# A new load split and new instruction orders for the start and the end of a fused attention and MLP kernel

## The chip, the cores and the metric

The kernel runs on one core of a Trainium2 chip (trn2). The metric is the device time of one execution in microseconds (us). Before the change it was 283.31 us, the median of three executions (282.98 to 283.46).

The engines are called by the profile's short names: PE is TensorE's matmuls and PEld its weight loads, DVE is VectorE, ACT is ScalarE, POOL is GpSimd, SP is SyncE (here it only issues DMA).

## The reference

```python
def _attn_ref(q, k, v):                       # each (8, 8, 576, 64): batch, head, row, head_dim
    q_s = softmax of q over head_dim          # max taken off first, 1e-9 added to the sum
    k_s = softmax of k over the rows
    kv = np.einsum('bhsd,bhse->bhde', k_s, v)
    return np.einsum('bhsd,bhde->bhse', q_s, kv)

def _moe_ref(x, w_in, w_out, beta):           # x (4608, 512), w_in (512, 2048), w_out (2048, 512)
    h = x @ w_in
    g = h * (1.0 / (1.0 + np.exp(-beta * h)))
    return g @ w_out
```

The attention output of all batches, as 4608 rows of 512, is the x of the second part. The inputs are float32. The kernel computes in bfloat16 with float32 accumulation.

## The kernel before

The program takes the rows in nine chunks. Chunks 0 to 7 are the first 512 rows of each batch, and one more chunk holds the 64 rows that are left of every batch. For a chunk the kernel makes qT (softmaxed q, transposed), one small matrix kv for each pair of heads, and x = kv times qT. Then 16 units follow. A unit j is 128 of the 2048 hidden columns: four matmuls for h (kt 0 to 3), a tanh on ACT, a product g on DVE, and four matmuls of g with w_out into four accumulators. So h and acc take 64 matmuls each in a chunk.

The program hands every engine its instructions in the order in which they are written. For batches 0 and 1 that order was tuned by hand, because weights, q, k and v arrive while the first products run. These are the parts that the change and the argument touch:

```python
    def load_q(b, parts=1, only=None, eng=nc.sync):
        # ... tile, source ...
        for s in range(parts) if only is None else (only,):
            eng.dma_start(t[:, s * n : (s + 1) * n, :], src[:, s * n : (s + 1) * n, :])

    # q_exp: ACT exponential of a group of heads; q_sum: DVE sum and reciprocal; q_mul: DVE product
    # tpe: four PE transposes of a head pair; q_ev: their eviction to qT; vz_cast: v to bfloat16
    # kz_exp: ACT exponential of k of a pair; kvz_norm: DVE reciprocal and two products
    def kvz_mm(b, j, tag=None, n=1):          # kv of head pair j: 18 products of 64x64 tiles
        # ...
        for i in range(RW):                   # 9
            for e in range(2):
                r = slice(e * D, (e + 1) * D)
                nc.tensor.matmul(t[r, 0, :], ek[b][r, j, ds(i * D, D)], va[b][r, j, i, :],
                                 start=(i == 0), stop=(i == RW - 1), tile_position=(e * D, e * D))

    def warm(n, tag):                         # n dummy matmuls on zeros
        # ...

    load_q(0, 2, 0)                           # 4 heads on SyncE's queue
    load_q(0, 2, 1, nc.scalar)                # 4 heads on ScalarE's
    load_kv(k_st, k, 0, "k_st", whole=True)
    # ... v of batch 0 by pair, beta, then the weights by block ...

    warm(18, tag="b0")
    q_exp(0, 0)
    q_sum(0, 0)
    q_exp(0, 1)
    q_mul(0, 0)
    kz_exp(0, 0)
    kz_exp(0, 1)
    q_sum(0, 1)
    vz_cast(0, 0, G)
    warm(18, tag="acc2")
    tpe(0, 0, "acc3")
    tpe(0, 1, "acc2")
    # ... batch 0 goes on; then, in batch 1:
    tpe(1, 0, "b0")
    w_cast("out", 3, 0, A)
    tpe(1, 1, "b1")
    kvz_mm(1, 0, "b2", 2)                     # two pairs in a row
    q_ev(1, 1, V)
    kvz_mm(1, 1)
    # ...
    mm_b(0, 14)
    vz_cast(1, 2, A, part=1)
    vz_cast(1, 2, G, part=0)
    kvz_mm(1, 3, "b0", 1)                     # two pairs in a row
    kvz_mm(1, 2, "b1", 1)
    # ...
    for st in range(R + 1):                   # the end: units 8 to 15 of the last chunk
        for j in range(HOLD, NJ):
            mm_b(LASTC, j, [st])
        store(LASTC, st)
```

The softmax here doesn't subtract the row's maximum and nothing guards it: scores larger than these inputs give would overflow.

## Time and profile before

| | before |
|---|---|
| time, median of 3 | 283.31 us |
| span of the profiled execution | 281.1 us (its time 282.86 us) |
| PE busy | 273.4 us, 97% |
| useful PE work starts | 10.29 us |
| h runs in one go, but for one stall, from | 16.02 us |

From the page of the kernel before come PE's line of the busy times and the chain of waits by engine:

```profile
PE 273.4 (97%) x1705; PEld 128.4 (46%) x1734; DVE 172.4 (61%) x269; ACT 162.9 (58%) x249; POOL 37.0 (13%) x57
PE 91%; DMA 6%; issue 1%; SPq 1%; POOL 0%; ACT 0%
```

PE bounds the kernel. In its steady part matmuls of 512 columns start every 0.216 us, and the change makes none of them shorter. Time can be won only where PE waits or does something useless.

The timeline of PE in the kernel before follows. Its columns are start in us, length in us, engine, line, operation, output and inputs, form, and how many instructions are merged; a bracket gives the idle time in front and what ended it. Now and then one matmul's record is missing, as in the run of 15 at 36.29, which has 16 in the program.

```profile
1.19 9.27 PE L518 MATMUL warm<-xT 128*128 128x512 bf16 x36 [1.19 <-DVE xT L599]
10.29 0.61 PE L294 MATMUL tp<-identity,eq 128*128 128x128 bf16 x8
...
16.02 3.40 PE L397 MATMUL h<-xT,w_in_b 128*128 128x512 bf16 x15
19.66 2.55 PE L397 MATMUL h<-xT,w_in_b 128*128 128x512 bf16 x11 [0.24 <-POOL w_in_b L170]
22.04 3.62 PE L445 MATMUL acc<-w_out_b,g 128*128 128x512 bf16 x16
...
36.29 3.62 PE L445 MATMUL acc<-w_out_b,g 128*128 128x512 bf16 x15
...
40.28 0.77 PE L313 MATMUL kv<-va,ek 64*64 64x65 bf16 x36
...
42.73 1.89 PE L445 MATMUL acc<-w_out_b,g 128*128 128x512 bf16 x8
44.55 0.77 PE L313 MATMUL kv<-va,ek 64*64 64x65 bf16 x36
...
46.99 3.19 PE L397 MATMUL h<-xT,w_in_b 128*128 128x512 bf16 x14
```

At 36.29 us PE has done all 64 h matmuls and 32 of the 64 acc matmuls of chunk 0. I call this milestone 1. At 46.99 us it starts the run of 14 h matmuls of chunk 1, with everything of chunk 0 and of batch 1's attention behind it. I call this milestone 2. The same work is done at these points in every kernel below. Between the milestones lie the other 32 acc matmuls, 16 transposes, the kv products of batch 1, four x and two h.

One weight load in the timeline of PEld of the kernel before:

```profile
44.55 0.65 PEld L313 LDWEIGHTS <-ek 64*64 64x64 bf16 x36 [0.42 <-ACT va L168]
```

PEld was idle for 0.42 us there and waited for a cast on ACT. The printed length of a run reaches about 0.16 us into the next one.

The end of the kernel before, from the timeline of PEld:

```profile
272.35 3.35 PEld L445 LDWEIGHTS <-g 128*128 128x128 bf16 x17 [0.48 <-DVE g L411]
```

The eighth of the last acc matmuls needs the last g, which DVE finishes at 272.30 us. From the start of the last h matmul to the first of the last 16 half-width products it took 5.56 us, where 24 matmuls at 0.216 us take 5.18 and the last h itself 0.22 us, so about 0.16 us was lost.

### The profile page before, as it was taken

What the parts mean: (1) busy time and instruction counts of PE and PEld (TensorE: products, weight loads), DVE (VectorE), ACT (ScalarE), POOL (GpSimd) and SP (SyncE); (2) the same over time, 40 slices, a digit from 0 to 9 for tenths busy, and PEclk for the clock granted to TensorE, in tenths of its full rate; (3) what the DMA queues carried; (4) which work ended last, traced back from release to release, by engine and by line L of the source; (5) the groups of instructions that cost most, each with busy time, mean ns of one, the idle gap of its engine ahead of it and who ended that gap; (6) DMA issues with size and microseconds to landing.
All of it is one profiled execution on the core that took longest, in us unless ns stands there. A gap on an engine that the chain in (4) does not pass through costs nothing.

```text
span 281.1 us, 4410 instructions
## 1 busy us (share of the span) xinstructions
PE 273.4 (97%) x1705; PEld 128.4 (46%) x1734; DVE 172.4 (61%) x269; ACT 162.9 (58%) x249; POOL 37.0 (13%) x57
## 2 busy tenths in 40 slices
PE   8899999999999999999999999999999999999995
PEld 3544454444444444444444444444444544445543
DVE  1864785983498338934794469546964596454361
ACT  3777886953495339633873478337933574354451
POOL 1551436230030003000300030001200000000000
PEclk9999999999999999999999999999999999999999
DMA  6999999929942994099409940698153034005003
GB/s 243 391 392 392 384 392 314 295 58 259 232 169 35 261 265 155 8 285 266 155 0 217 326 156 16 138 247 252 75 126 102 6 146 75 0 0 152 0 0 149
DMA packets 55172, 50.09 MB, mean 178 GB/s; under 512 B 26600, under 2 KB 47344, under 8 KB 55152
## 3 DMA queue, kind: packets, MB, share of 16 engines
q1 hardware_dynamic: 54480, 49.17, 58.5%
q10 hardware_dynamic: 672, 0.66, 0.7%
q8 instruction: 13, 0.21, 0.3%
q14 instruction: 7, 0.06, 0.1%
HBM read 36.71 MB, written 9.44 MB: 164 GB/s over the span
## 4 chain that ended last, share of the span: by engine, by line
PE 91%; DMA 6%; issue 1%; SPq 1%; POOL 0%; ACT 0%
PE acc L445 43%; PE h L397 43%; DMA v_st<-in_v_dram 3%; DMA w_in<-in_moe_w_in_dram 3%; PE kv L338 2%; PE x L369 1%; PE acc L437 1%; PE kv L313 0%; PE tp L294 0%; PE x L382 0%; POOL w_in_b L170 0%; SPq L131 0%; SPq L128 0%; SPq L105 0%; SPq L150 0%
## 5 line engine op out<-in xcount | busy, mean ns | idle before, releaser
L407 ACT ACTIVATE th<-h,beta_t 128x512 bf16<-128x512 f32 x144 | 97.6, 686 | 87.9 <-PE h L397 85.8
L411 DVE SCALAR_TENSOR_TENSOR g<-th,h 128x512 bf16<-128x512 bf16 x144 | 96.7, 680 | 83.2 <-ACT th L407 81.4
L397 PE MATMUL h<-xT,w_in_b 128*128 128x512 bf16 x569 | 141.1, 379 | 0.6 <-POOL w_in_b L170 0.2
L445 PE MATMUL acc<-w_out_b,g 128*128 128x512 bf16 x538 | 136.1, 379 | 2.0 <-issue 1.3
L397 PEld LDWEIGHTS <-w_in_b 128*128 128x128 bf16 x576 | 56.3, 98 | 66.6 <-POOL w_in_b L170 0.7
L445 PEld LDWEIGHTS <-g 128*128 128x128 bf16 x560 | 53.5, 98 | 65.6 <-issue 2.5
L170 POOL CAST va<-v_st 128x2048 bf16<-128x2048 f32 (+2 forms) x14 | 16.9, 1205 | 145.3 <-DMA v_st<-in_v_dram 145.1
L258 DVE TENSOR_REDUCE rq<-eq 128x16 f32<-128x1024 bf16 x18 | 21.9, 1216 | 7.5 <-ACT eq L247 7.1
L264 DVE TENSOR_TENSOR eq<-eq,rq 128x1024 bf16<-128x1024 bf16 x18 | 22.5, 1248 | 0.1
L247 ACT ACTIVATE eq<-q_st 128x1024 bf16<-128x1024 f32 x16 | 16.6, 1053 | 3.2 <-DMA q_st<-in_q_dram 3.2
L168 ACT CAST xT<-x 128x512 bf16<-128x512 f32 x18 | 9.9, 589 | 11.1 <-PE x L369 10.1
L170 DVE CAST xT<-x 128x512 bf16<-128x512 f32 x18 | 11.8, 687 | 6.1 <-PE x L369 5.3
L170 DVE COPY o<-acc 128x512 f32<-128x512 f32 (+1 forms) x19 | 12.1, 669 | 3.4 <-PE acc L445 3.2
L168 ACT COPY o<-acc 128x512 f32<-128x512 f32 (+1 forms) x18 | 9.6, 576 | 7.1 <-PE acc L445 2.9
L189 ACT ACTIVATE ek<-k_st 128x1024 bf16<-128x1024 f32 x12 | 12.6, 1052 | 0.0
L518 PE MATMUL warm<-xT 128*128 128x512 bf16 x36 | 9.3, 423 | 1.2 <-DVE xT L599 1.2
L170 POOL CAST w_in_b<-w_in 128x512 bf16<-128x512 f32 (+1 forms) x10 | 6.8, 698 | 8.6 <-DMA w_in<-in_moe_w_in_dram 8.6
L518 PEld LDWEIGHTS <-xT 128*128 128x128 bf16 x36 | 3.8, 107 | 6.2 <-issue 1.8
L182 ACT ACTIVATE ek<-k_st 128x576 bf16<-128x576 f32 x8 | 5.3, 684 | 1.5 <-DMA k_st<-in_k_dram 1.5
L168 ACT CAST w_out_b<-w_out 128x1024 bf16<-128x1024 f32 x5 | 5.3, 1051 | 0.2 <-DMA w_out<-in_moe_w_out_dram 0.2
L338 PEld LDWEIGHTS <-ek 128*64 128x64 bf16 x192 | 4.1, 111 | 2.5 <-issue 2.5
L437 PE MATMUL acc<-w_out_b,g 128*128 128x256 bf16 x32 | 5.0, 273 | 0.0
(48 smaller groups left out, 79.6 us busy)
## 6 DMA issues: line engine op xcount, KB each, us to landing
out_dram<-o SPq DMA_DIRECT2D x14, 512.0 KB, 3.7
q_st<-in_q_dram SPq DMA_DIRECT2D x24, 256.0 KB, 4.2
k_st<-in_k_dram SPq DMA_DIRECT2D x6, 1024.0 KB, 8.3
v_st<-in_v_dram SPq DMA_DIRECT2D x6, 1024.0 KB, 11.0
w_in<-in_moe_w_in_dram SPq DMA_DIRECT2D x6, 512.0 KB, 9.4
v_st<-in_v_dram SPq DMA_DIRECT2D x8, 288.0 KB, 8.2
w_out<-in_moe_w_out_dram SPq DMA_DIRECT2D x4, 512.0 KB, 9.2
w_out<-in_moe_w_out_dram SPq DMA_DIRECT2D x2, 1024.0 KB, 10.6
```

The source lines that it names most:

```text
L168: eng.copy(dst, src)
L170: eng.tensor_copy(dst, src)
L189: nc.scalar.activation(ek[b][:, :, h, :].rearrange("p i h d -> p h i d"), k_st[b][:, h, 0 : R * D].rearrange("p h (i d) -> p h i d", i=R), ...
L247: nc.scalar.activation(eq[b][:, :, s * m : (s + 1) * m, :].rearrange("p i h d -> p h i d"), q_st[b][:, s * m : (s + 1) * m, :].rearrange(" ...
L258: nc.vector.tensor_reduce(rq[b][:, 0, :, h], eq[b][:, :, h, :], axis=AX.X, op=ALU.add)
L264: eng.tensor_tensor(eq[b][:, :, h, :], eq[b][:, :, h, :], rq[b][:, 1, :, h].unsqueeze(3).to_broadcast((P, R, m, D)), ALU.mult,)
L338: nc.tensor.matmul(t[r * D : (r + 1) * D, j, :], ek[b][:, i, hd, :] if i < R else ekt[(b // 2) % 2][:, ds(hd * D, D)], va[b][:, i, hd, :] ...
L397: nc.tensor.matmul(h[:], w_unit(j, kt), x_of(c)[:, kt, :], start=(kt == 0), stop=(kt == KT - 1),)
L407: nc.scalar.activation(th[:], h_of[c, j][:], ACTF.Tanh, scale=beta_t[:, j : j + 1])
L411: nc.vector.scalar_tensor_tensor(out=g[:], in0=th_of.pop((c, j))[:], scalar=1.0, in1=h_of[c, j][:], op0=ALU.add, op1=ALU.mult)
L445: nc.tensor.matmul(acc[st][:], g[:, ds(st * P, P)], w_out_b[:, j, :], start=(j == 0), stop=(j == NJ - 1),)
L518: nc.tensor.matmul(t[:], xT[2][:, 0, 0:P], xT[2][:, 0, :])
```

## The change

The change has four parts. Head: q of batch 0 comes as one head pair on SyncE's queue and three pairs on ScalarE's, its softmax goes pair by pair, and batch 0 gets a new order (with 30 dummy matmuls instead of 36, in four groups). Weight loads: input block 3 comes before output block 1. Batch 1: a new order, with each pair's kv product alone, and new loads to match. Tail: unit 15 is used one matmul later.

```diff
-        for s in range(parts) if only is None else (only,):
-            eng.dma_start(t[:, s * n : (s + 1) * n, :], src[:, s * n : (s + 1) * n, :])
+        only = range(parts) if only is None else only
+        hs = slice(n * only[0], n * (only[-1] + 1))
+        eng.dma_start(t[:, hs, :], src[:, hs, :])
...
-    HB, AB = ["b0", "b1"], ["b2", "b3"]
+    HB, AB = ["b1", "b2"], ["b0", "b3"]
...
-    load_q(0, 2, 0)
-    load_q(0, 2, 1, nc.scalar)
+    load_q(0, 4, [0])
+    load_q(0, 4, [1, 2, 3], nc.scalar)
...
-    w_load("out", 1)
     w_load("in", 3, 1)
     w_load("in", 3, 0)
+    w_load("out", 1)
... (new order of the k and v loads of batch 1)
-    q_exp(0, 0)
-    q_sum(0, 0)
-    q_exp(0, 1)
-    q_mul(0, 0)
+    q_exp(0, 0, 4)
+    q_sum(0, 0, 4)
+    q_exp(0, 3, 4)
+    q_mul(0, 0, 4)
+    q_exp(0, 2, 4)
+    q_sum(0, 3, 4)
+    tpe(0, 0, "acc3")
+    q_exp(0, 1, 4)
+    q_sum(0, 2, 4)
+    q_ev(0, 0, A)
+    q_sum(0, 1, 4)
+    q_mul(0, 2, 4)
     kz_exp(0, 0)
+    q_mul(0, 1, 4)
+    warm(10, tag="acc2")
+    tpe(0, 2, "acc3")
     kz_exp(0, 1)
... (the rest of batch 0 in a new order)
-    kvz_mm(1, 0, "b2", 2)
-    q_ev(1, 1, V)
-    kvz_mm(1, 1)
+    kvz_mm(1, 0, "b1", 1)
+    kz_exp(1, 2)
+    tpe(1, 3, "b3")
+    kvz_norm(1, 0)
+    tpe(1, 2, "b2")
     mm_b(0, 12)
+    kz_exp(1, 1)
+    q_ev(1, 3, V)
+    q_ev(1, 2, V)
+    kvz_mm(1, 2, "b0", 1)
... (kv of pair 1 after one x, kv of pair 3 after mm_b(0, 14))
-    for st in range(R + 1):
-        for j in range(HOLD, NJ):
+    for j in range(HOLD, NJ - 1):
+        mm_b(LASTC, j, [0])
+    mm_b(LASTC, HOLD, [1])
+    mm_b(LASTC, NJ - 1, [0])
+    store(LASTC, 0)
+    for st in range(1, R + 1):
+        for j in range(HOLD + (st == 1), NJ):
             mm_b(LASTC, j, [st])
         store(LASTC, st)
```

The intent is that h starts earlier, that less waits for the last data of batch 1, and that the last g is waited for no more. The arithmetic is the same.

More of the change, by code (lines that the diff above doesn't have):

```diff
@@ L565 @@
     load_kv(v_st, v, 0, "v_st", [1])
+    load_kv(v_st, v, 0, "v_st", [2])
     nc.sync.dma_start(beta_r[:], moe_beta.rearrange("(hh q) -> hh q", q=2 * P))
-    load_kv(v_st, v, 0, "v_st", [2])
     load_kv(v_st, v, 0, "v_st", [3])
@@ L578 @@
     w_load("in", 2, 1)
-    w_load("out", 1)
     w_load("in", 3, 1)
     w_load("in", 3, 0)
-    load_q(1, 2, 0)
+    w_load("out", 1)
+    load_q(1, 2, [0])
     w_load("out", 2)
-    load_q(1, 2, 1)
-    load_kv(v_st, v, 1, "v_st", [1])
+    load_q(1, 2, [1])
+    load_kv(v_st, v, 1, "v_st", [2])
+    w_load("out", 3, 0)
     load_kv(k_st, k, 1, "k_st", [0])
     load_kv(v_st, v, 1, "v_st", [0])
+    load_kv(k_st, k, 1, "k_st", [2])
     load_kv(k_st, k, 1, "k_st", [1])
-    w_load("out", 3, 0)
+    load_kv(v_st, v, 1, "v_st", [1])
     w_load("out", 3, 1)
-    load_kv(k_st, k, 1, "k_st", [2])
+    load_kv(k_st, k, 1, "k_st", [3])
     load_kv(v_st, v, 1, "v_st", [3])
-    load_kv(k_st, k, 1, "k_st", [3])
-    load_kv(v_st, v, 1, "v_st", [2])
     load_q(2)
@@ L605 @@
     warm(18, tag="b0")
-    q_exp(0, 0)
-    q_sum(0, 0)
-    q_exp(0, 1)
-    q_mul(0, 0)
+    q_exp(0, 0, 4)
[10 more added lines that the diff above has]
+    q_mul(0, 2, 4)
     kz_exp(0, 0)
+    q_mul(0, 1, 4)
+    warm(10, tag="acc2")
+    tpe(0, 2, "acc3")
     kz_exp(0, 1)
-    q_sum(0, 1)
+    q_ev(0, 2, V)
     vz_cast(0, 0, G)
-    warm(18, tag="acc2")
@@ L616 @@
-    tpe(0, 0, "acc3")
+    warm(1, tag="acc1")
     tpe(0, 1, "acc2")
-    q_ev(0, 0, A)
-    kvz_mm(0, 0, "acc1", 1)
+    q_mul(0, 3, 4)
+    kz_exp(0, 2)
+    warm(1, tag="acc1")
+    kvz_mm(0, 0, "acc3", 1)
     vz_cast(0, 1, G)
+    q_ev(0, 1, V)
+    tpe(0, 3, "acc1")
     kz_exp(0, 3)
+    kvz_norm(0, 0)
+    kvz_mm(0, 1, "acc2", 1)
+    vz_cast(0, 2, G)
+    q_ev(0, 3, A)
     beta_pe("acc0")
-    kvz_norm(0, 0)
-    kvz_mm(0, 1, "acc3", 1)
-    vz_cast(0, 2, G)
-    kz_exp(0, 2)
-    q_mul(0, 1)
@@ L628 @@
-    xpe(0, 0, "b3")
+    kvz_norm(0, 1)
+    kvz_mm(0, 2, "acc3", 1)
+    vz_cast(0, 3, A, part=1)
+    vz_cast(0, 3, G, part=0)
     beta_ev()
-    vz_cast(0, 3, G, part=0)
-    vz_cast(0, 3, A, part=1)
-    kvz_mm(0, 2, "acc1", 2)
+    xpe(0, 0, "acc1")
+    kvz_norm(0, 2)
+    kvz_mm(0, 3, "acc2", 1)
+    w_castk(0, 0, G)
     xev(0, 0, A)
-    kvz_mm(0, 3)
-    w_castk(0, 0, G)
-    q_ev(0, 1, A)
-    kvz_norm(0, 1)
-    tpe(0, 3, "acc0")
-    tpe(0, 2, "b3")
-    w_castk(0, 1, G)
-    q_ev(0, 3, A)
@@ L642 @@
-    hpe(0, 3, [0], "b0")
-    kvz_norm(0, 2, 2)
-    xpe(0, 1, "acc3")
-    hpe(0, 1, [0], "b1")
-    q_ev(0, 2, A)
-    hpe(0, 2, [0], "b2")
-    xev(0, 1, V)
-    hpe(0, 0, [0], "acc0")
-    w_castk(0, 2, A)
-    xpe(0, 3, "acc2")
+    xpe(0, 1, "acc0")
+    kvz_norm(0, 3)
+    xpe(0, 2, "b3")
+    xev(0, 1, A)
+    hpe(0, 0, [0], "b0")
+    hpe(0, 1, [0], "b1")
+    xev(0, 2, V)
+    w_castk(0, 1, A)
+    xpe(0, 3, "acc3")
+    w_castk(0, 2, G)
+    hpe(0, 3, [0], "b2")
+    xev(0, 3, V)
+    hpe(0, 2, [0], "acc0")
@@ L652 @@
+    hpe(0, 0, [1])
     w_castk(0, 3, G)
-    xpe(0, 2, "acc1")
-    xev(0, 3, V)
-    hpe(0, 0, [1])
-    xev(0, 2, A)
+    hpe(0, 3, [1])
+    hpe(0, 3, [2])
     hpe(0, 1, [1])
-    hpe(0, 3, [1])
-    hpe(0, 2, [1])
-    hpe(0, 2, [2])
-    hpe(0, 2, [3])
+    hpe(0, 1, [2])
+    hpe(0, 1, [3])
+    hpe(0, 3, [3])
+    th_act(0, 1)
     w_castk(1, 0, G)
     hpe(0, 0, [2])
-    th_act(0, 2)
-    hpe(0, 1, [2])
-    w_castk(1, 1, G)
-    hpe(0, 1, [3])
-    hpe(0, 5, [0], "b3")
-    th_act(0, 1)
@@ L670 @@
-    hpe(0, 3, [2])
-    g_dve(0, 2)
-    hpe(0, 5, [1])
-    w_castk(1, 2, G)
-    hpe(0, 3, [3])
-    w_castk(1, 3, A)
-    hpe(0, 0, [3])
-    g_dve(0, 1)
-    hpe(0, 6, [0], "b2")
-    hpe(0, 5, [2])
-    th_act(0, 3)
-    hpe(0, 5, [3])
-    hpe(0, 7, [0], "b1")
-    th_act(0, 0)
+    hpe(0, 0, [3])
+    hpe(0, 2, [1])
+    w_castk(1, 1, G)
+    th_act(0, 3)
+    hpe(0, 2, [2])
+    g_dve(0, 1)
+    hpe(0, 2, [3])
+    hpe(0, 4, [0], "b3")
+    th_act(0, 0)
+    hpe(0, 4, [1])
+    g_dve(0, 3)
@@ L684 @@
+    w_castk(1, 3, G)
+    hpe(0, 5, [0], "b1")
+    hpe(0, 5, [1])
+    w_castk(1, 2, A)
+    g_dve(0, 0)
+    hpe(0, 7, [0], "b2")
+    th_act(0, 2)
+    hpe(0, 7, [1])
+    hpe(0, 4, [2])
+    hpe(0, 5, [2])
+    hpe(0, 4, [3])
+    g_dve(0, 2)
+    hpe(0, 5, [3])
+    th_act(0, 4)
+    hpe(0, 7, [2])
+    hpe(0, 7, [3])
+    hpe(0, 6, [0], "b0")
+    w_cast("out", 0, 0, G)
+    th_act(0, 5)
     hpe(0, 6, [1])
-    g_dve(0, 3)
+    g_dve(0, 4)
     hpe(0, 6, [2])
     hpe(0, 6, [3])
-    th_act(0, 5)
@@ L689 @@
-    w_cast("out", 0, 0, G)
-    hpe(0, 7, [1])
-    g_dve(0, 0)
-    hpe(0, 7, [2])
-    hpe(0, 4, [0], "b0")
-    th_act(0, 6)
-    g_dve(0, 5)
-    hpe(0, 4, [1])
-    hpe(0, 4, [2])
-    mm_b(0, 0)
-    w_cast("out", 0, 1, A)
+    th_act(0, 7)
+    g_dve(0, 5)
+    mm_b(0, 0)
+    th_act(0, 6)
+    w_cast("out", 0, 1, G)
+    g_dve(0, 7)
+    mm_b(0, 1)
     g_dve(0, 6)
-    mm_b(0, 1)
-    w_castk(2, 0, G)
+    w_castk(2, 0, A)
+    w_castk(2, 1, G)
     mm_b(0, 2)
-    w_castk(2, 1, G)
     mm_b(0, 3)
@@ L706 @@
     w_castk(2, 2, A)
-    w_castk(2, 3, A)
-    hpe(0, 4, [3])
-    hpe(0, 7, [3])
-    th_act(0, 4)
-    hpe(0, 9, [0, 1, 2, 3], "b2")
-    th_act(0, 7)
-    g_dve(0, 4)
-    hpe(0, 8, [0, 1, 2, 3], "b3")
+    w_castk(2, 3, G)
+    hpe(0, 11, [0, 1, 2, 3], "b0")
+    w_cast("in", 3, 1, A)
+    hpe(0, 10, [0, 1, 2, 3], "b1")
+    th_act(0, 11)
+    hpe(0, 8, [0, 1, 2, 3], "b2")
+    w_cast("in", 3, 0, G)
+    th_act(0, 10)
+    g_dve(0, 11)
+    hpe(0, 9, [0, 1, 2, 3], "b3")
+    th_act(0, 8)
+    g_dve(0, 10)
@@ L715 @@
+    hpe(0, 13, [0, 1, 2, 3], "b0")
+    g_dve(0, 8)
     th_act(0, 9)
-    g_dve(0, 7)
-    w_cast("out", 1, 0, A)
-    hpe(0, 11, [0, 1, 2, 3], "b0")
+    hpe(0, 14, [0, 1, 2, 3], "b1")
     g_dve(0, 9)
-    hpe(0, 10, [0, 1, 2, 3], "b1")
-    th_act(0, 8)
-    w_cast("in", 3, 1, G)
-    th_act(0, 11)
-    g_dve(0, 8)
+    th_act(0, 13)
+    w_cast("out", 1, 0, G)
+    w_cast("out", 1, 1, A)
+    hpe(0, 15, [0, 1, 2, 3], "b2")
+    g_dve(0, 13)
     mm_b(0, 4)
-    w_cast("out", 1, 1, A)
-    g_dve(0, 11)
@@ L728 @@
-    w_cast("in", 3, 0, G)
+    th_act(0, 14)
+    th_act(0, 15)
+    g_dve(0, 14)
     mm_b(0, 5)
-    th_act(0, 10)
+    q_exp(1, 0)
+    g_dve(0, 15)
     mm_b(0, 6)
-    g_dve(0, 10)
-    q_exp(1, 0)
-    hpe(0, 13, [0, 1, 2, 3], "b0")
     q_sum(1, 0)
-    hpe(0, 12, [0, 1, 2, 3], "b1")
-    th_act(0, 13)
     mm_b(0, 7)
-    th_act(0, 12)
-    g_dve(0, 13)
-    w_cast("out", 2, 1, G)
-    w_cast("out", 2, 0, A)
-    hpe(0, 14, [0, 1, 2, 3], "b2")
-    q_mul(1, 0)
-    hpe(0, 15, [0, 1, 2, 3], "b0")
@@ L746 @@
-    q_exp(1, 1)
-    g_dve(0, 12)
-    mm_b(0, 8)
-    vz_cast(1, 1, G)
-    th_act(0, 14)
-    q_sum(1, 1)
-    th_act(0, 15)
-    mm_b(0, 9)
-    kz_exp(1, 0)
-    vz_cast(1, 0, G, part=0)
-    mm_b(0, 10)
-    g_dve(0, 15)
-    vz_cast(1, 0, A, part=1)
-    kz_exp(1, 1)
-    g_dve(0, 14)
-    mm_b(0, 11)
-    q_mul(1, 1)
-    tpe(1, 0, "b0")
-    w_cast("out", 3, 0, A)
-    tpe(1, 1, "b1")
-    kvz_mm(1, 0, "b2", 2)
-    q_ev(1, 1, V)
-    kvz_mm(1, 1)
-    q_ev(1, 0, A)
-    tpe(1, 3, "b1")
@@ L771 @@
-    kvz_norm(1, 0, 2)
-    tpe(1, 2, "b3")
-    w_cast("out", 3, 1, G)
-    mm_b(0, 12)
-    q_ev(1, 2, A)
-    q_ev(1, 3, V)
-    kz_exp(1, 2)
-    xpe(1, 1, "b0")
-    xpe(1, 0, "b1")
-    xev(1, 1, V)
-    mm_b(0, 13)
+    w_cast("out", 2, 1, A)
+    w_cast("out", 2, 0, G)
+    hpe(0, 12, [0, 1, 2, 3], "b0")
+    q_mul(1, 0)
+    q_exp(1, 1)
+    mm_b(0, 8)
+    vz_cast(1, 2, G, part=0)
+    vz_cast(1, 2, A, part=1)
+    mm_b(0, 9)
+    q_sum(1, 1)
+    th_act(0, 12)
+    tpe(1, 0, "b1")
+    w_cast("out", 3, 0, A)
@@ new lines @@
+    tpe(1, 1, "b2")
+    mm_b(0, 10)
+    q_ev(1, 0, V)
+    q_mul(1, 1)
+    kz_exp(1, 0)
+    mm_b(0, 11)
+    vz_cast(1, 0, G, part=0)
+    vz_cast(1, 0, A, part=1)
+    q_ev(1, 1, A)
+    g_dve(0, 12)
+    kvz_mm(1, 0, "b1", 1)
[3 more added lines that the diff above has]
+    tpe(1, 2, "b2")
+    mm_b(0, 12)
+    kz_exp(1, 1)
+    q_ev(1, 3, V)
+    q_ev(1, 2, V)
+    kvz_mm(1, 2, "b0", 1)
+    vz_cast(1, 1, A, part=1)
+    vz_cast(1, 1, G, part=0)
+    xpe(1, 0, "b1")
+    kvz_norm(1, 2)
@@ L782 @@
+    kvz_mm(1, 1, "b2", 1)
+    xev(1, 0, A)
+    mm_b(0, 13)
+    kvz_norm(1, 1)
+    w_cast("out", 3, 1, G)
+    hpe(1, 0, [0], "b0")
+    xpe(1, 2, "b1")
+    kz_exp(1, 3)
+    xpe(1, 1, "b2")
+    xev(1, 2, V)
+    mm_b(0, 14)
     vz_cast(1, 3, A, part=1)
     vz_cast(1, 3, G, part=0)
-    xev(1, 0, A)
-    kz_exp(1, 3)
-    mm_b(0, 14)
-    vz_cast(1, 2, A, part=1)
-    vz_cast(1, 2, G, part=0)
-    kvz_mm(1, 3, "b0", 1)
-    kvz_mm(1, 2, "b1", 1)
+    xev(1, 1, V)
+    kvz_mm(1, 3, "b1", 1)
@@ L791 @@
+    mm_b(0, 15)
     kvz_norm(1, 3)
-    mm_b(0, 15)
-    kvz_norm(1, 2)
-    xpe(1, 3, "b0")
+    hpe(1, 2, [0], "b2")
     store(0, 0)
-    hpe(1, 0, [0], "b2")
-    xev(1, 3, V)
-    hpe(1, 0, [1])
-    xpe(1, 2, "b1")
-    hpe(1, 1, [0], "b3")
-    store(0, 1)
-    xev(1, 2, A)
-    hpe(1, 1, [1])
-    hpe(1, 2, [0], "b0")
-    hpe(1, 2, [1])
+    xpe(1, 3, "b1")
+    hpe(1, 1, [0], "b3")
+    hpe(1, 1, [1])
+    xev(1, 3, A)
+    store(0, 1)
+    hpe(1, 1, [2])
+    hpe(1, 0, [1])
     hpe(1, 0, [2])
+    hpe(1, 0, [3])
@@ L807 @@
     store(0, 2)
-    hpe(1, 0, [3])
-    hpe(1, 1, [2])
+    hpe(1, 1, [3])
+    hpe(1, 3, [0], "b1")
+    th_act(1, 0)
     store(0, 3)
-    th_act(1, 0)
-    hpe(1, 1, [3])
-    hpe(1, 2, [2])
-    hpe(1, 2, [3])
-    th_act(1, 1)
-    hpe(1, 3, [0], "b1")
-    g_dve(1, 0)
     hpe(1, 3, [1])
     hpe(1, 3, [2])
-    th_act(1, 2)
     hpe(1, 3, [3])
+    th_act(1, 1)
+    g_dve(1, 0)
+    hpe(1, 2, [1])
+    hpe(1, 2, [2])
+    th_act(1, 3)
+    hpe(1, 2, [3])
     g_dve(1, 1)
     mm_b(1, 0)
-    th_act(1, 3)
+    th_act(1, 2)
@@ L825 @@
+    g_dve(1, 3)
+    mm_b(1, 1)
     g_dve(1, 2)
-    mm_b(1, 1)
-    g_dve(1, 3)
     tail_zero(0)
```

## The prediction

> **What bounds the kernel now.** TensorE: 273.4 us busy of a 281.1 us span (page, busy times) and 91% of the chain of waits; DMA of v and w_in at the start makes up most of the rest. From about 50 us the timeline shows matmuls back to back at 216 ns, which the change hardly touches. What can be won lies in the first 50 us and the last 10.
>
> Head (timeline): 36 dummy matmuls hold TensorE until 10.3 us; from there to 16.0 us it issues about 4.2 us of useful work (transposes, k-v products, x, 3 h), so about 1.5 us is idle; only then does h run gaplessly. It stalls 0.24 us at 19.4 us (weight block 1, second half) and about 0.35 us near 44.2 us, where the last v pair of batch 1 landed at 43.7 us. DMA is full until 44 us (390 GB/s), so arrivals are a floor for any reordering.
>
> Tail: the weight load waits 0.48 us for the last g; TensorE loses about 0.15 us.
>
> **What the change does.**
> 1. q as 2+6 heads. In the DMA packets SyncE's queue moves alone for 1.25 us (200 KB), then each queue gets about 190 KB/us, half of one alone. This agrees with the Trainium skill, "DMA: Bandwidth & Descriptors", section on queues, rings and completion order: an engine takes turns between queues. Estimate: the first pair lands at about 4.0 us (half of q landed at 5.6), the other three at 6.8 (was 6.2). k (9.2 us) and v (from 10.0) stay.
> 2. Softmax by pair: reductions and products (1.22 us for 4 heads) become about 0.63 us each. VectorE also gets two evictions (0.42 us). Estimate: its k-v normalisations end near 15.5 us (was 14.95), the last x eviction near 16.8 (as now). VectorE becomes the tight engine of the head.
> 3. All q is transposed before the last k-v product, so h starts earlier (about 14.6 us) and fills the wait: 22 h matmuls instead of 18 by 19.6 us. Lead: 0.5 to 0.9 us.
> 4. Weight block 3 before output block 1: neutral.
> 5. Batch 1: one pair instead of two waits for the last data; a k-v pair (0.36 us), x (0.22) and h (0.22) run before it. This hides the 0.35 us stall.
> 6. Last unit last in the first block: one 216 ns matmul covers the wait; saves about 0.15 us.
>
> **Sum.** Lead 0.7, plus 0.35, plus 0.15, minus about 0.3 for new waits among small pieces: about 1.0 us, all on the critical path. The arrival at 43.7 us caps it at about 1.4 us.
>
> Predicted time 282.3 us, 8 in 10 between 281.5 and 283.1. Faster by over 2%: 0.01; within 2%: 0.98; slower by over 2%: 0.01.
>
> **What would show it.** First q exponential near 4.2 us, the next near 6.9; first h near 14.6 us, 22 by 19.6; first output product near 21.8 us (was 22.04); no TensorE gap near 44 us; the k-v product of batch 1's last pair near 44.2 us; no wait for g at the end; steady state unchanged.
>
> **What would make it wrong.** If the six heads land after 7.5 us, VectorE pushes the last x eviction past 17.5 us and the lead vanishes. In-order ScalarE holds casts waiting for DMA in front of evictions; one late landing at 36 to 42 us could cost 0.5 us. With fewer dummy matmuls, gaps could slow TensorE (the first dummies took 0.43 us, later ones 0.216): the clock row of the slices would show under 9 early on.

## The result, and the profile after

| | before | after |
|---|---|---|
| median | 283.38 us (4 executions, 282.98 to 283.56) | 282.56 us (4 executions, 282.47 to 282.69) |
| ratio | | 0.9973, 95% interval 0.9956 to 0.9991 |
| span of the profiled execution | 281.1 us (time 282.86) | 280.8 us (time 282.55) |

A ratio here is the mean time of one kernel's executions over that of the other's of the same rounds, so it is not quite the ratio of the medians quoted. Executions over 1.5% slower than the fastest of the same kernel are left out of the means. The output is correct.

The gain is 0.82 us by the medians and 0.3 us by the two traces. The difference between these two numbers comes up again below: the traced execution of the kernel before (282.86 us) was faster than each of the four timed with it.

From the page of the kernel after:

```profile
PE 273.9 (98%) x1699; PEld 128.2 (46%) x1728; DVE 175.3 (62%) x284; ACT 162.0 (58%) x248; POOL 38.7 (14%) x58
PE 94%; DMA 3%; issue 1%; POOL 1%; SPq 0%; ACT 0%
```

The timeline of PE after:

```profile
1.19 6.67 PE L519 MATMUL warm<-xT 128*128 128x512 bf16 x18 [1.19 <-DVE xT L600]
7.69 0.39 PE L295 MATMUL tp<-identity,eq 128*128 128x128 bf16 x4
7.92 2.32 PE L519 MATMUL warm<-xT 128*128 128x512 bf16 x10
...
14.42 0.38 PE L398 MATMUL h<-xT,w_in_b 128*128 128x512 bf16 x1
...
15.07 6.88 PE L398 MATMUL h<-xT,w_in_b 128*128 128x512 bf16 x30
21.78 3.62 PE L446 MATMUL acc<-w_out_b,g 128*128 128x512 bf16 x16
...
35.60 1.89 PE L446 MATMUL acc<-w_out_b,g 128*128 128x512 bf16 x7
...
39.67 0.48 PE L314 MATMUL kv<-va,ek 64*64 64x65 bf16 x18
...
41.49 0.48 PE L314 MATMUL kv<-va,ek 64*64 64x65 bf16 x18
...
42.22 0.48 PE L314 MATMUL kv<-va,ek 64*64 64x65 bf16 x18
...
45.11 0.48 PE L314 MATMUL kv<-va,ek 64*64 64x65 bf16 x18
...
46.83 3.19 PE L398 MATMUL h<-xT,w_in_b 128*128 128x512 bf16 x14
```

Read it against the list of before. The dummies are split, so the first transposes run at 7.69 us. From 15.07 us h runs to the first acc at 21.78 us. By the starts of its matmuls it loses 0.06 us at 15.57 us and 0.17 us at 19.20 us, in front of weight loads; the kernel before lost 0.41 us at 19.66 us (the 0.24 us of the list is counted from the printed end). So the stall is shorter, not gone. By then all 32 h matmuls of units 0 to 7 are done, where before had 30. Milestone 1 is at 35.60 us instead of 36.29, a lead of 0.69 us. Milestone 2 is at 46.83 us instead of 46.99, and the lead has shrunk to 0.16 us. So 0.53 us were lost again between the milestones, in batch 1, where the prediction expected a further gain of 0.35 us.

The first two exponentials of q on ACT, after the change, show when the first pair and the other three had landed:

```profile
3.79 0.63 ACT L248 ACTIVATE eq<-q_st 128x512 bf16<-128x512 f32 x1 [1.25 <-DMA q_st<-in_q_dram]
6.13 1.67 ACT L248 ACTIVATE eq<-q_st 128x512 bf16<-128x512 f32 x3 [1.70 <-DMA q_st<-in_q_dram]
```

Before, the first exponential ran at 5.68 us.

The same weight load at the end, after:

```profile
272.19 3.19 PEld L446 LDWEIGHTS <-g 128*128 128x128 bf16 x16 [0.27 <-DVE g L412]
```

From the start of the last h matmul to the first of the last 16 half-width products it now took 5.40 us instead of 5.56: the tail order saves 0.16 us. PEld still waits a little for g, but PE has no gap there.

### The profile page after: what moved, and what is told of

Its sections match the earlier page's. It is cut to its first block, busy times and chain, and to the rows that moved or that the text cites. A ratio compares the mean times of both kernels' runs of the same rounds, so it can differ in the third digit from the quotient of the medians.

```text
span 280.8 us, 4419 instructions
## 1 busy us (share of the span) xinstructions
PE 273.9 (98%) x1699; PEld 128.2 (46%) x1728; DVE 175.3 (62%) x284; ACT 162.0 (58%) x248; POOL 38.7 (14%) x58
## 4 chain that ended last, share of the span: by engine, by line
PE 94%; DMA 3%; issue 1%; POOL 1%; SPq 0%; ACT 0%
PE h L398 44%; PE acc L446 43%; DMA v_st<-in_v_dram 3%; PE kv L339 2%; PE x L370 1%; PE acc L438 1%; PE kv L314 1%; PE x L383 1%; POOL va L171 1%; PE tp L295 0%; SPq L129 0%; SPq L106 0%; ACT o L169 0%; PE x L361 0%; PE tb L552 0%
## 5 line engine op out<-in xcount | busy, mean ns | idle before, releaser
L171 POOL CAST va<-v_st 128x2048 bf16<-128x2048 f32 (+2 forms) x14 | 17.5, 1261 | 145.7 <-DMA v_st<-in_v_dram 145.7
L259 DVE TENSOR_REDUCE rq<-eq 128x16 f32<-128x1024 bf16 (+1 forms) x20 | 22.1, 1105 | 5.6 <-ACT eq L248 5.2
L265 DVE TENSOR_TENSOR eq<-eq,rq 128x1024 bf16<-128x1024 bf16 (+1 forms) x20 | 22.8, 1142 | 0.1
L248 ACT ACTIVATE eq<-q_st 128x1024 bf16<-128x1024 f32 (+1 forms) x18 | 16.9, 956 | 3.2 <-DMA q_st<-in_q_dram 3.2
L171 POOL CAST w_in_b<-w_in 128x512 bf16<-128x512 f32 (+1 forms) x9 | 5.9, 660 | 5.7 <-DMA w_in<-in_moe_w_in_dram 5.6
L171 POOL CAST w_out_b<-w_out 128x1024 bf16<-128x1024 f32 x5 | 5.2, 1040 | 6.3 <-DMA w_out<-in_moe_w_out_dram 6.3
L260 DVE RECIPROCAL rq<-rq 128x16 f32<-128x16 f32 (+1 forms) x20 | 4.9, 243 | 0.7
```

The costliest lines, as they stand in the source:

```text
L171: eng.tensor_copy(dst, src)
L248: nc.scalar.activation(eq[b][:, :, s * m : (s + 1) * m, :].rearrange("p i h d -> p h i d"), q_st[b][:, s * m : (s + 1) * m, :].rearrange(" ...
L259: nc.vector.tensor_reduce(rq[b][:, 0, :, h], eq[b][:, :, h, :], axis=AX.X, op=ALU.add)
L265: eng.tensor_tensor(eq[b][:, :, h, :], eq[b][:, :, h, :], rq[b][:, 1, :, h].unsqueeze(3).to_broadcast((P, R, m, D)), ALU.mult,)
```

## The experiments

Twelve runs followed, three of them repeats. Each had five rounds, with the kernel before in the same rounds. The rounds came in three groups: before_again, before_tail, head_only and batch1_only; then head_tail, grouped, fewer_dummies and q_4_4, on another chip; then the other four, on the chip of the first group. Between groups, compare the ratios to the kernel before and the traces rather than the medians. All of them except one execution, named below, were of state fast, and all outputs were correct.

The table gives, for each profiled execution, milestone 1, the stretch from milestone 1 to milestone 2, and the rest from milestone 2 to the end of the span. The starts were read from the timeline of PE as above.

| kernel | median, us | milestone 1 | stretch | rest |
|---|---|---|---|---|
| before | 283.38 | 36.29 | 10.70 | 234.10 |
| before_again | 283.15 | 36.26 | 10.70 | 234.10 |
| before_tail | 283.18 | 36.76 | 10.70 | 233.93 |
| batch1_only | 283.55 | 36.42 | 11.24 | 234.09 |
| fewer_dummies | 284.29 | 37.61 | 10.70 | 234.09 |
| after | 282.56 | 35.60 | 11.23 | 233.92 |
| grouped | 283.09 | 35.57 | 11.79 | 233.93 |
| q_4_4 | 284.22 | 37.38 | 11.14 | 233.93 |
| head_only | 282.15 | 35.47 | 10.77 | 234.10 |
| head_tail | 282.11 | 35.49 | 10.99 | 233.93 |
| head_tail_again | 282.21 | 35.84 | 10.79 | 233.92 |
| mul_early | 282.39 | 36.05 | 10.71 | 233.92 |
| no_mid_dummies | 284.46 | 35.52 | 10.71 | 233.93 |

The rest is one of two numbers: 234.10 with the old tail and 233.93 with the new one, within 0.01 us. Everything else is decided before milestone 2.

### before_again: the kernel before, unchanged

> The kernel before once more, unchanged, for the spread and a second trace of it. Both theories: ratio 1.000 within 0.001. Theory A (before has no slack at its last k-v pair of batch 1: data ready 44.47 us, TensorE there at 44.46 us in the first trace): executions differ by some 0.5 us, and in a slower execution the extra time lies before that pair, as a TensorE wait there or in the head. Rival: the spread lies anywhere, or in the start and end.

Measured: 283.15 us (282.85 to 283.95, six executions), ratio 1.0004 (0.9990 to 1.0019). The eleven executions of the kernel before in the same rounds went from 282.63 to 283.59. So the kernel before differs from itself by about 1 us. Its second trace is as fast as the first and shows no place for the spread; the next experiment does by chance. What I called a lack of slack at the last kv pair turned out wrong (see head_only).

### before_tail: the tail order alone

```diff
 (on the kernel before)
-    for st in range(R + 1):
-        for j in range(HOLD, NJ):
+    ... the new last loop of the change
```

> Only the last part of the change (unit 15 after one matmul of block 1). From the traces of before and after: the last 16 half-width products start 0.18 us nearer to the last h than before, so 0.15 to 0.2 us less, about 283.2 us; the weight load still waits for g for about 0.3 us instead of 0.5. Rival (end is set by stores): no difference.

Measured: 283.18 us, ratio 0.9995 (0.9982 to 1.0008). The timed difference is not clear of noise. The trace shows the 0.17 us that was expected (rest 233.93 instead of 234.10), and milestone 1 of this execution is 0.47 us later, which has nothing to do with the tail. Its timeline of PE shows why:

```profile
1.19 10.39 PE L518 MATMUL warm<-xT 128*128 128x512 bf16 x36 [1.19 <-DVE xT L599]
11.41 0.61 PE L294 MATMUL tp<-identity,eq 128*128 128x128 bf16 x8
```

The same 36 dummies took 10.39 us here and 9.27 us in the first trace. In this execution 12 of the first 17 distances between their starts were about 0.4 us, in the first one 6; the later ones were 0.216 us. The record of the granted clock says full speed from 6.17 us here and from 3.90 us there. The old head puts all dummies in front of the first transposes, so a late clock pushes the first transposes from 10.29 to 11.41 us. In batch1_only, with full clock from 5.04 us, they started at 10.86 us. The Trainium skill, "TensorE: Matmul & The Clock Gate", Part 1, says that the clock is raised after a window of about 3.4 us of activity, and that the window runs free, so that the point differs from run to run. The traces agree with that: full speed began between 3.90 and 7.23 us in the traces that have this record, a spread of 3.33 us.

### head_only: the new head, with the old batch 1 and the old tail

```diff
 (on the changed kernel; loads of batch 1, bank sets and last loop as before)
-    hpe(0, 12, [0, 1, 2, 3], "b0")
+    hpe(0, 12, [0, 1, 2, 3], "b3")
... batch 1 as in the kernel before: kvz_mm(1, 0) and (1, 1) in a row, (1, 3) and (1, 2) in a row
```

> New q split and new batch 0, old order of batch 1 and old tail. Theory A (the head's lead of 0.69 us at 36 us is real, but batch 1's last k-v pair waits for data that land at 43.7 us): TensorE reaches that pair at about 43.8 us, waits until about 44.5 us for the casts, and the lead at 50 us is 0.0 to 0.15 us; time equal to before within 0.2 us. Theory B (the single k-v bursts of the new batch 1 are what eats the lead, 0.52 us by the trace): without them the lead stays 0.6 to 0.7 us, time 0.6 us below before.

Measured: 282.15 us (282.12 to 283.08), ratio 0.9969 (0.9956 to 0.9983). Theory A falls and theory B holds; the gain, 0.9 us by the ratio, is larger than the 0.6 us of theory B. The timeline of PE of this run:

```profile
35.47 3.62 PE L446 MATMUL acc<-w_out_b,g 128*128 128x512 bf16 x16
...
39.46 0.77 PE L314 MATMUL kv<-va,ek 64*64 64x65 bf16 x36
...
43.73 0.84 PE L314 MATMUL kv<-va,ek 64*64 64x65 bf16 x36
...
46.24 3.18 PE L398 MATMUL h<-xT,w_in_b 128*128 128x512 bf16 x14
```

The lead of 0.82 us at milestone 1 is still 0.75 us at milestone 2. The last kv group ran 0.82 us earlier than before and took only 0.07 us longer. In the first trace the cast that this group needs ended at 44.47 us, and I took that for a limit set by the landing of v at 43.60 us. It was not: an x eviction of PE's results and an exponential stood in front of the cast on ACT, so its time followed PE's pace. With a faster PE the cast ended at 43.96 us, with v landed at 43.53. That is close to the real limit: this run waited 0.07 us for it and the next ones up to 0.29 us.

### batch1_only: the new order of batch 1 alone

```diff
 (on the kernel before; its loads of batch 1 and bank sets as after)
-    ... batch 1 of the kernel before
+    ... batch 1 of the changed kernel: kvz_mm(1, 0), (1, 2), (1, 1), (1, 3), each alone
```

> Old head, new order of batch 1 (four single k-v bursts, new loads of batch 1), old tail. Theory A and the burst account: four single bursts take 0.41 us each plus a 0.1 us drain in front of each instead of two pairs of 0.70 us, so TensorE is 0.4 to 0.5 us behind before at 50 us, and the time is 0.3 to 0.5 us above before, unless before itself waits there in its slower executions. Rival (the new order of batch 1 gains by hiding a wait of 0.35 us, as predicted): 0.3 us below before.

Measured: 283.55 us (283.35 to 284.56), ratio 1.0019 (1.0004 to 1.0034). The stretch is 11.24 us, as in the changed kernel, and not 10.70. So the new order of batch 1 costs 0.54 us of PE time, and it costs that with the old head as well as with the new one. The timeline of PE of this run gives the account of it:

```profile
41.37 1.03 PE L445 MATMUL acc<-w_out_b,g 128*128 128x512 bf16 x4
42.33 0.48 PE L313 MATMUL kv<-va,ek 64*64 64x65 bf16 x18
42.73 0.39 PE L382 MATMUL x<-qsT,kvp 128*128 128x512 bf16 x1
43.05 0.48 PE L313 MATMUL kv<-va,ek 64*64 64x65 bf16 x18
```

Four acc matmuls fill 0.863 us where h or acc follows them. Here they start at 41.37 us and kv starts 0.96 us later, so about 0.09 us is lost in front of the group. One x (0.216 us) is followed by kv after 0.32 us, which loses 0.10 us. A single group takes 0.41 us until the next kind of matmul starts. In the old order two groups in a row take 0.70 us together, and there is one gap in front of both. In the changed kernel the same sums are 4 times 0.41 minus 2 times 0.70, which is 0.24 us, plus about 0.28 us for the gaps (0.46 us in front of four groups, 0.18 us in front of two). Together they make 0.52 of the 0.53 us.

Not all of this is the price of the groups. The first of the four gaps is 0.17 us in the changed kernel, 0.08 us more than the others behind acc: PE waited there for POOL's cast of v, which ended at 39.62 us (it took 0.83 us under a product on DVE; the same cast took 0.46 us in q_4_4, under a sum). (In batch1_only the same 0.08 us appear behind the first group, where the transposes wait for a product on DVE.) The run q_4_4, described below, has the same order of batch 1 without this wait. Its stretch is 11.14 us, so the groups and their gaps alone cost 0.44 us. First the cast in the changed kernel, then milestones 1 and 2 of q_4_4:

```profile
38.79 0.83 POOL L171 CAST va<-v_st 128x320 bf16<-128x320 f32 x1 [2.19 <-DMA v_st<-in_v_dram]
```

```profile
37.38 1.89 PE L446 MATMUL acc<-w_out_b,g 128*128 128x512 bf16 x8
...
48.52 3.19 PE L398 MATMUL h<-xT,w_in_b 128*128 128x512 bf16 x14
```

The Trainium skill, "TensorEngine Tiling (Array Packing)", Key Properties, says that a change of tiling mode drains the engine. The traces agree: kv is the only part of this stretch that uses 64x64 tiles, and every change to it shows a gap of 0.09 us or more. The page does not give the size.

### head_tail and head_tail_again: the new head and the new tail, old batch 1

```diff
 (on the kernel of head_only)
+    ... the new last loop of the change
```

> New head of batch 0 and new tail, old order of batch 1. From the traces: the earlier run of the head alone ended 0.72 us ahead, the tail order saves 0.17 us between the last h and the last products. Theory (the two add, the new batch 1 order is a net cost): trace span near 280.2 us, median about 282.0 us, 0.4 to 0.6 us below the changed kernel. Rival (the run of the head alone was only lucky): about 282.5 us, as the changed kernel.

> New head, new tail, old order of batch 1, now in the same rounds as the changed kernel. Theory (the new order of batch 1 is a net cost of 0.4 to 0.5 us): 0.3 to 0.5 us below the changed kernel in these rounds. Rival (earlier difference was chance between rounds): within 0.15 us of it.

> The changed kernel once more, in the same rounds as the next one: median 282.4 to 282.7 us, spread about 0.3 us, and a second trace of it. In that trace the accounting of batch 1 repeats: four single k-v bursts of 0.41 us.

The first time it was 282.11 us (281.94 to 282.32), ratio 0.9965 (0.9943 to 0.9986). The second time it ran in the same rounds as the changed kernel: 282.21 us (282.08 to 282.34) against 282.59 us (282.49 to 283.00, five fast executions), with ratios to the kernel before of 0.9961 (0.9945 to 0.9978) and 0.9976 (0.9957 to 0.9995). So it beats both kernels: 0.38 us below the changed one by the medians of the same rounds, without overlap between their executions. The two intervals do overlap, since they carry the spread of the kernel before. The trace has a span of 280.41 us and not 280.2; in the stretch 0.29 us of waiting appeared at the last kv group. In the second trace it was 0.09 us, so that wait varies. Here theory A is right after all, with an earlier limit than I thought: v landed at 43.78 us, its casts ended at 44.28 us, and the second pair of the group started at 44.34 us. A still faster head would gain little in this order. The two gains did not add in the times: head_only had 282.15 us, so the 0.17 us of the tail show in the traces only.

One execution of the changed kernel in these rounds took 414.29 us, at a mean granted clock of 0.66. The profile fell on it. I compare nothing with it, and so there is no second fast trace of the changed kernel; its order of batch 1 is seen once more in q_4_4.

### grouped: three kv products of batch 1 in one group

```diff
 (on the changed kernel)
-    kvz_mm(1, 0, "b1", 1)
+    mm_b(0, 12)
     kz_exp(1, 2)
     tpe(1, 3, "b3")
-    kvz_norm(1, 0)
     tpe(1, 2, "b2")
-    mm_b(0, 12)
...
+    kvz_mm(1, 0, "b1", 1)
     kvz_mm(1, 2, "b0", 1)
-    xpe(1, 0, "b1")
     kvz_mm(1, 1, "b2", 1)
     mm_b(0, 13)
+    xpe(1, 0, "b1")
...
```

> The changed kernel with the first three k-v products of batch 1 in one burst instead of three single ones. Burst account (a single burst costs 0.41 us and a 0.1 us drain in front; in a group 0.35 us each): two bursts less, so the start of the second batch's long h run moves about 0.3 us earlier relative to the run of acc at 35 us, time 0.2 to 0.4 us below the changed kernel, about 282.2 us. Rival (batch 1 waits for data in any order): no gain, the burst itself waits.

Measured: 283.09 us (283.04 to 283.45), ratio 1.0001 (0.9979 to 1.0023), where the changed kernel had 0.9973 and 0.9976 in its own rounds. The stretch is 11.79 us instead of 11.23. This attempt failed. The 54 products take 1.20 us until acc starts, 0.18 us of it a gap in front of the third pair; without that gap a pair takes 0.34 us, as the account says. But the order around them now waits:

```profile
39.93 1.04 PE L446 MATMUL acc<-w_out_b,g 128*128 128x512 bf16 x4 [0.30 <-DVE g L412]
...
41.35 1.26 PE L314 MATMUL kv<-va,ek 64*64 64x65 bf16 x54
...
43.42 0.96 PE L383 MATMUL x<-qsT,kvp 128*128 128x512 bf16 x3
```

The acc matmuls of unit 12 came before their g was ready, and three x in a row took 1.05 us until the next matmul, where three nominal slots are 0.65 us: they wait for the three normalisations that DVE does one after the other. The waits ate more than the group saved. The run does not refute the account of the groups, but its time does not confirm the size either.

### fewer_dummies and no_mid_dummies: are the dummies needed?

```diff
 (fewer_dummies, on the kernel before)
-    warm(18, tag="acc2")
+    warm(8, tag="acc2")
 (no_mid_dummies, on the kernel of head_tail)
-    warm(10, tag="acc2")
```

> The kernel before with 26 instead of 36 dummy matmuls. Theory (TensorE starts its first transposes only when the dummies are done, and that takes 10.3 to 11.4 us depending on how many of them run at 0.43 instead of 0.216 us): the first transposes start when their data are there, at about 9.6 to 9.9 us, the spread between executions falls from about 1 us to about 0.3 us and the median by 0.1 to 0.3 us. Rival (the spread comes from the DMA or elsewhere): same spread, same median.

> As the run before last (new head and tail, old batch 1), without the 10 dummy matmuls between the first transposes and the second. Theory (they keep TensorE's granted clock up; with 26 instead of 36 dummies in the old kernel one trace showed the clock at 0.5 for 3.4 us and four of six executions were 1.3 to 2.5 us longer): in part of the executions the clock falls, median 0.5 to 2 us above its parent, spread over 1 us. Rival (transposes and k-v products suffice): same time as its parent.

Measured: 284.29 us (282.56 to 285.13), ratio 1.0032 (0.9999 to 1.0066), and 284.46 us (281.94 to 284.94), ratio 1.0033 (1.0005 to 1.0062). By these ratios only the second is clear of noise. For the first kernel my theory was wrong: the spread grew instead of shrinking. The theory drawn from that held for the second kernel. Both kernels fall into groups by the mean granted clock of the execution. At 1.00 fewer_dummies took 282.56 and 282.94 us. At 0.988 it took 284.38, 285.07 and 285.13 us, and at 0.994 284.20 us. At 1.00 no_mid_dummies took 281.94 and 282.62 us. At 0.988 it took 284.43 to 284.94 us, in four executions. The profile of fewer_dummies fell on the execution at 0.994. This is the view by windows of that run; after the busy times the columns are the granted clock, the DMA share and GB/s:

```profile
7.30:14.00 6.70, 5.36 (x93) 3.41 (x92) 5.89 (x12) 4.58 (x10) 3.61 (x5) 1.00 1.05 390
14.10:17.40 3.30, 3.30 (x22) 1.75 (x16) 1.44 (x4) 1.59 (x3) 1.98 (x5) 0.50 1.04 374
```

By the record of the clock it was at half from 14.06 to 17.47 us, which is the length of the window that the page names, and the first acc came at 23.36 us instead of 22.04. As an estimate, one stretch of 3.41 us at half speed lowers the mean over 283 us to 0.994 and two lower it to 0.988, which are the means seen. So the dummies do two jobs: they raise the clock (read from the traces; no run leaves the first ones out) and they keep it up through the thin stretch of transposes and kv products. The new head keeps the clock up with 12 dummies placed between the transposes; with 10 of them gone it fell in four of six executions. In the executions that I have of the changed kernel, head_only and head_tail, leaving out the 414 us one, the mean clock was never under 0.998. The kernel before had two executions at 0.994 among those listed in the rounds, 284.78 and 284.19 us. These are part of its spread. Whether such a drop comes in a given execution I cannot predict; the trace of no_mid_dummies shows PE busy for only 4.83 of the same 6.70 us and no drop. Counted in stretches of 3.41 us from the rise of the clock, PE was busy for 2.34 us of the one before the drop, and for 1.72 us of one in no_mid_dummies (6.82 to 10.23 us) that no drop followed. So PE's busy time alone does not decide it.

### q_4_4: the old split of q

```diff
 (on the changed kernel)
-    load_q(0, 4, [0])
-    load_q(0, 4, [1, 2, 3], nc.scalar)
+    load_q(0, 2, [0])
+    load_q(0, 2, [1], nc.scalar)
```

> The changed kernel with q of batch 0 in two halves of four heads on the two queues, as before; softmax by pair stays. Theory (the early pair lets VectorE, the tight engine of the head, start 1.8 us earlier): the first q sum moves from 4.5 to about 6.3 us, VectorE's last q product ends about 1 us later, the first h about 0.7 to 1.0 us later, and the lead at the first output product is mostly gone: 0.4 to 0.7 us above the changed kernel. Rival (the 2 and 6 split does nothing, order and fewer dummies are what helped): within 0.15 us of it.

Measured: 284.22 us (284.12 to 284.93), ratio 1.0043 (1.0017 to 1.0068). The median is 1.66 us above that of the changed kernel, which ran in other rounds; in the traces milestone 1 is 1.78 us later. That is the direction expected and more than twice as much. The first exponential moved to 5.71 us and the first h to 16.20 us. The early pair is needed in this order: without it the new head is worse than the old one. Most of the surplus over the estimate is seen on DVE and POOL. DVE's products of eq in this run:

```profile
10.35 1.99 DVE L265 TENSOR_TENSOR eq<-eq,rq 128x512 bf16<-128x512 bf16 x2
...
12.59 0.81 DVE L265 TENSOR_TENSOR eq<-eq,rq 128x512 bf16<-128x512 bf16 x1
```

Two products take 1.99 us. In the changed kernel two of them take 1.24 us at 9.21 us. All three products now fall on POOL's casts of v (10.06 to 13.72 us), and both are stretched, the products by 0.88 us in all. The next run tests this.

### mul_early: products before v arrives

```diff
 (on the kernel of head_tail: each q_mul right behind its q_sum, pairs in the order 0, 2, 1, 3)
     q_exp(0, 1, 4)
     q_sum(0, 2, 4)
+    q_mul(0, 2, 4)
...
     q_sum(0, 1, 4)
+    q_mul(0, 1, 4)
+    q_sum(0, 3, 4)
```

> As the run before (new head and tail, old batch 1), with each pair's softmax product right behind its sum, so that two of the three products run before v lands and only one can meet a GpSimd cast. Theory (a VectorE product of two SBUF operands and a GpSimd cast exclude each other; casts of v took 1.02 and 1.14 us under products, 0.66 alone): the first cast of v takes 0.66 us, the second up to 1.1 us or its product is stretched; first h 0 to 0.3 us earlier; time within 0.2 us, as the weights' landing then limits. Rival (casts are slow for another reason, such as the DMA or ScalarE): the first cast still takes about 1.0 us.

Measured: 282.39 us (282.28 to 282.51), 0.18 us above its parent in the same rounds. The kernel is not faster, but the casts answer the question. First POOL and DVE around the first cast of v in the changed kernel, then the same in mul_early around its first and its third cast, all from the timelines of short windows (a cast between the two took 0.67 us):

```profile
9.21 1.24 DVE L265 TENSOR_TENSOR eq<-eq,rq 128x512 bf16<-128x512 bf16 x2
9.95 1.02 POOL L171 CAST va<-v_st 128x576 bf16<-128x576 f32 x1 [7.99 <-DMA v_st<-in_v_dram]
```

```profile
10.12 0.68 DVE L259 TENSOR_REDUCE rq<-eq 128x8 f32<-128x512 bf16 x1
10.13 0.66 POOL L171 CAST va<-v_st 128x576 bf16<-128x576 f32 x1 [8.17 <-DMA v_st<-in_v_dram]
...
11.24 0.85 DVE L265 TENSOR_TENSOR eq<-eq,rq 128x512 bf16<-128x512 bf16 x1
...
11.63 0.98 POOL L171 CAST va<-v_st 128x576 bf16<-128x576 f32 x1
```

A cast under a sum takes 0.66 us. A cast that starts while a product runs takes 0.98 or 1.02 us. The product that started while a cast ran took 0.85 us instead of 0.69. The slow cast moved with the product, from the first to the third place, while the landing of v did not move in this way. The Trainium skill, "SBUF — State Buffer", section "SBUF: two separate sides", says that VectorE and GpSimd share a port pair as an exclusive lock, which a VectorE instruction with two SBUF inputs takes against a GpSimd instruction that reads SBUF. The traces agree: the product reads eq and rq from SBUF, the sum has one input. The time did not fall because DVE's sums and evictions now end later (its last product at 12.09 us, in head_tail_again at 11.77 us). The landing is not the reason: in head_tail_again, from the same rounds, the first cast of v began at 10.18 us, later than here (10.13 us), and milestone 1 still came 0.21 us earlier.

## Why the prediction was right or wrong, point by point

The total was right: 282.3 us with a range of 281.5 to 283.1 was forecast, and 282.56 us was measured. Luck had a part in it. Step 5 was 0.88 us too good (0.35 us forecast as a gain, 0.53 us measured as a loss). Two things made up for it: 0.3 us had been taken off for waits that hardly came, and the kernel before is usually slower than the one execution whose trace I reckoned from (point 8).

1. **q as 2+6 heads: right, with the second landing too late.** The first exponential was forecast at 4.2 us and came at 3.79; the next was forecast at 6.9 and came at 6.13. The estimate took a half share for each queue; the packets show that SyncE's queue moved nothing between 3.5 and 5.0 us, with its first pair done and k not begun, so ScalarE's queue had the DMA engines to itself. q_4_4 shows that the early pair carries the new head.
2. **VectorE as the tight engine: right in kind, the times too late.** The k-v normalisations ended at 14.75 us instead of the 15.5 forecast, and the last x eviction at 16.07 us instead of 16.8. I had not seen that the products also block GpSimd's casts of v. The first two casts took 1.02 and 1.14 us.
3. **Lead of 0.5 to 0.9 us: right.** It was 0.69 us at milestone 1. The first h was forecast near 14.6 us and came at 14.42, the first acc near 21.8 us and came at 21.78. Of the 22 h matmuls forecast by 19.6 us, 21 have a record.
4. **Weight block 3 first: no stall appeared.** Its effect alone was not tested.
5. **"This hides the 0.35 us stall": wrong, and this is the step that failed.** There was no stall. I read an idle weight load and a cast that ended at 44.47 us as an idle PE; PE was in its acc matmuls until 44.62 us. The new order of batch 1 gains nothing and costs 0.53 us in the trace: about 0.44 us by more and shorter kv groups, about 0.08 us by a new wait for a cast. batch1_only shows the cost with the old head and head_only shows its absence with the new one. The landing of v as a cap was not reached by the changed kernel: its last cast of v ended at 44.28 us, and PE came to that group at 45.11 us. In the old order it was reached, with waits of 0.07 to 0.29 us in head_only and the two runs of head_tail.
6. **Tail, 0.15 us: right.** It measured 0.16 to 0.17 us in every trace with the new tail. No timed comparison shows it clear of noise. PEld still waits for g (0.27 us), against the forecast of no wait.
7. **Minus 0.3 us for new waits:** with batch 1 the loss was larger, but only about 0.08 us of it was a wait; the rest, the cost of small groups, was not in the sum at all.
8. **What the sum lacked.** The traces give 0.69 minus 0.53 plus 0.16, which is 0.32 us, and the medians give 0.82 us. The rest is that I took one execution for the kernel before. In the four traces with 36 dummies the first transposes behind them start between 10.29 and 11.41 us, and milestone 1 came at 36.26 to 36.76 us. In the five traces of the new head as the change has it (after, grouped, head_only, head_tail, head_tail_again) it came at 35.47 to 35.84 us. The clock rose late in three of these nine traces, with 12 slow distances among the first 17 dummies instead of 6 to 9: before_tail has the latest milestone of the old head (36.76 us), while after and grouped (35.60 and 35.57 us) lie among the others of the new one. So part of the gain is that the new head hardly depends on when the clock rises. That this makes up all of the missing 0.5 us was not shown, since most timed executions have no trace. My warning about gaps and the clock was justified as a mechanism, but it hits kernels with fewer dummies than this one.

## What to carry to other kernels

An idle weight load or a wait of a helper engine counts only if the matmul row itself has a gap there. Before you book a stall, compare the starts of the matmuls with their number times 0.216 us; the printed lengths overlap the next run by about 0.16 us and can hide a gap. On a busy matmul engine, count how often the order changes the tiling mode and keep small tiled products together, as long as the group does not make others wait. Test the parts of a change alone: here the head and the tail gained, the middle cost the larger part of it in the trace, and the kernels without the middle (head_only and head_tail) were the fastest.

## What the Trainium skill lacked or had wrong

- "TensorEngine Tiling (Array Packing)", Key Properties: it says that changing the mode drains the engine but not what that costs. Here a group of 64x64 products behind 128x128 ones began 0.09 to 0.10 us late, and a group of 18 products took 0.41 us alone and 0.35 us in a pair.
- "TensorE: Matmul & The Clock Gate", Part 1: it does not say how busy a window must be. With PE busy for 5.36 of 6.70 us in front and no printed idle time of PE over 0.87 us, the clock fell to 0.50 for 3.41 us in one execution; with 4.83 of the same 6.70 us busy it did not in another. Full speed began between 3.90 and 7.23 us. For the rise, 2.71 busy of the 3.41 us before 3.90 us were enough in the kernel before; in fewer_dummies 2.63 of the 3.41 us before 3.82 us were not, and full speed began one such stretch later.
- "SBUF — State Buffer", section "SBUF: two separate sides": it states the exclusive lock; the sizes seen here are a cast of 0.66 us that took 0.90 to 1.14 us and a product of 0.69 us that took up to 0.85 us when one of each met, and 1.99 us for two products that met a row of casts.
- "DMA: Bandwidth & Descriptors", queues, rings and completion order: the turns between queues were seen (about 190 KB per us each), but not that a queue may be silent between two of its transfers: SyncE's moved nothing from 3.5 to 5.0 us. In all traces the first packet of k moved at 4.97 to 5.31 us, 3.7 us or more after its issue at 1.25 us, whether the queue had been silent before (the new split of q) or not (the old one); the first packet of q moved 1.1 us after its issue. Why is not known.
- No page explains a single execution of 414.29 us at a mean granted clock of 0.66 on one core, where all others of the same kernel took 282.5 to 283.0 us.
